# Attention with normed heads and a SiLU layer, in fp32: reciprocals spread in one round of DMAs, and whole products in the fillers of couples 4 to 8

## The chip, the cores and the metric

The program runs on one core of a Trainium2 chip. The metric is the device time of one execution in microseconds. Three runs of the kernel before took 1308.16, 1308.67 and 1309.16 us, so its median is 1308.67 us. Everything is computed in 32-bit floats.

The core's engines each work through their own list of instructions in order: PE (TensorE, matmuls), DVE (VectorE), ACT (ScalarE), POOL (GpSimd) and SP (SyncE, which here only issues DMAs). They wait for each other by semaphores.

## The reference

Two blocks follow each other: an attention with root-mean-square normed queries and keys, and a two-layer block with SiLU between.

```python
q, k, v: (8, 12, 448, 64)      # batch, heads, sequence, head dimension
def rmsnorm(x, g):
    return x / np.sqrt(np.mean(x * x, axis=-1, keepdims=True) + 1e-06) * g
q_n, k_n = rmsnorm(q, g_q), rmsnorm(k, g_k)
scores = 1.0 / np.sqrt(64) * np.matmul(q_n, k_n.transpose(0, 1, 3, 2))
attn = np.exp(scores - np.max(scores, axis=-1, keepdims=True))
attn = attn / (np.sum(attn, axis=-1, keepdims=True) + 1e-09)
out = np.matmul(attn, v)                         # (8, 12, 448, 64)
x = out.transpose(0, 2, 1, 3).reshape(3584, 768)
h = x @ w_in                                     # w_in: (768, 2048)
g = h * (1.0 / (1.0 + np.exp(-h)))
result = g @ w_out                               # w_out: (2048, 768)
```

## The kernel before

**Couples.** The 96 heads (8 batches of 12) are taken four at a time, as 24 "couples" of two pairs. Six couples (GROUP) make a group, the attention of two batches. For couple c, `visit(c)` computes the scores (L741, matmuls of 64 x 64), their exponentials on ACT (L746) and the product with v (L778); the last part of couple c-1's product with v, and its division by the row sums (L841, `divide`), lie in the visit of c. `between(c)` then prepares the next couple: it transposes queries and keys, adds up the exponentials (`add`, L792 on DVE; `sum_up`, L816, a matmul with ones on PE), takes the reciprocals (L825, in two halves on DVE) and spreads them.

**Spreading the reciprocals.** The sums come out as 32 rows for each combination of head h and pair i. `factors(c)` is a pair of tiles, one for each pair i, in which the reciprocals have to stand in both halves of the rows of a head. `spread` (L827 to L834) does so by DMAs of 32 x 448: four into the second tile (L832), and after these have landed, two within the first tile (L834). All are issued by SP, save that in couple 5 half of them go through POOL's queue.

**Fillers.** PE's work in the attention depends on ACT and DVE, so independent matmuls are put between: the first layer, x @ w_in, of the group before. They are products of Strassen's kind, seven for a block of 2 x 2 (class `Seven`: `two` makes products 1 and 2, `five` makes 6, 5, 7, 3 and 4). A product is three steps (HW), a step is one 128 x 128 x 448 fp32 matmul (two records in the trace, L940). The result of a product is emptied out of PSUM by DVE (`plus`, L890: an addition to a part already there) or by ACT (a copy, L948 or L958). In `five`, POOL adds product 5 to two parts (L960, L961), and products 3 and 4 are added to what results. `fill(others, prompt)` emits so many steps as are due (`filler["share"]`), and deals other work out between them. There are two fills in each `between`, except in couple 5, which has only one, before the group's end. From couple 6 on a fill is 13 steps, from 12 on 14. In couples 3 (second fill) to 5, `make_ahead` makes the products 1 and 2 of two blocks ahead, at 2.4 steps a fill.

**Where a product stands.** PSUM has two banks named "mm" for products, two places of two banks named "sc" (scores, transposes, sums from couple 6 on) and two for the product with v. `bank` gives a product an "mm" bank, or every second time an "sc" place if a flag allows: `turns["third"]`, set from couple 8 on, and only while more than five steps are due. In couples 8 to 10 it is off in the second fill.

**Generators.** A product yields after every step. The code that empties it stands after its last yield, so the emptying of a product that ends a fill is emitted when the next fill, or the work between, asks for a step.

**Other work.** `sum_x` (L887) adds parts of x, the left operands of the products. `Rounder` turns w_in (and w_out), which come as 64-bit words, into fp32: `load` (SP, L88), `open` (two ACT passes, L103 and L104), `round` (three DVE instructions, L126, L129, L133, and one on POOL, L137). `halves` says which of these come in which fill. `norm` squares, sums and scales the queries and keys: squares on ACT (L472), sums on DVE (L473), a power on POOL (L501), scaling (L516) for couple 7's q on POOL. `pair_up` (L726) writes a few small blocks by POOL before couple 8. After couple 23 the second layer's products ("deep", L1247 and L1284) run until the end.

All of this order is written out by hand: the instructions of an engine are those of the program text, in its order.

## Time and profile before

| | us |
|---|---|
| median of three runs | 1308.67 |
| the profiled execution | 1308.39 |
| its span | 1306.6 |
| PE busy | 1290.7 |
| DVE busy | 949.3 |
| ACT busy | 502.4 |
| POOL busy | 363.0 |

The granted clock of PE was 0.999 of full speed. The span is the time from the first to the last instruction of the profiled execution; the device time is 1.8 us more. A line of the timeline reads: start, duration, engine, source line, operation, the tile written and the tiles read, shapes, count, and in brackets how long the engine had been idle and what it waited for. "SPq" is SP issuing a DMA. Neighbouring instructions of one kind are put together, with their count behind the x. The attention, with its fillers, takes until about 725 us; couple 4's fills lie at 86.1 and 91.2 us, couple 5's at 110.6, couple 6's at 126.7 and 140.1, couple 7's at 162.0 and 173.5, couple 8's at 196.0 and 207.7, couple 9's at 230.1 and 241.0, couple 10's at 262.7 and 274.3.

### The profile page before, as it was taken

Reading aid. Unit: us, or ns where it says so; the run is one execution under the profiler, and the core shown is the slowest. Engines: PE = TensorE matmul, PEld = TensorE weight load, DVE = VectorE, ACT = ScalarE, POOL = GpSimd, SP = SyncE. Lnnn points to the kernel's source line nnn. Section 1 sums busy time; section 2 is a strip of 40 time slices with the busy share of each in tenths; the row PEclk is TensorE's granted clock in tenths of the full one; section 3 lists DMA queues with packets and bytes.
Section 4 is the critical chain, followed back from the end, with each engine's and each line's share of the span. In section 5 each row is a group of like instructions: output and inputs, shape, how many; then the busy total and the mean of one; then the engine's idle time right before and its main releaser. Section 6 shows DMA issues by size and latency. Waiting matters only on the chain.

```text
span 1306.6 us, 19889 instructions
## 1 busy us (share of the span) xinstructions
PE 1290.7 (99%) x7174; PEld 828.7 (63%) x7174; DVE 949.3 (73%) x1628; ACT 502.4 (38%) x880; POOL 363.0 (28%) x227
## 2 busy tenths in 40 slices
PE   8999999999999999999999999999999999999998
PEld 4444444444444444444444455558999999999998
DVE  6988777867555556755554786698978787878785
ACT  7866656655444545545534344310100000100000
POOL 6765555443334333334321244300000000000000
PEclk9999999999999999999999999999999999999999
DMA  8774347545444443444321457312323223231411
GB/s 209 194 194 134 102 98 189 129 99 124 95 97 93 123 95 89 111 106 93 87 77 48 155 178 260 117 61 83 102 83 101 89 90 102 76 127 51 137 42 40
DMA packets 267967, 146.32 MB, mean 112 GB/s; under 512 B 204356, under 2 KB 251748, under 8 KB 267860
## 3 DMA queue, kind: packets, MB, share of 16 engines
q1 hardware_dynamic: 267200, 143.80, 39.9%
q8 instruction: 59, 0.97, 0.3%
q0 software_dynamic: 352, 0.96, 0.2%
q14 instruction: 48, 0.39, 0.1%
q10 hardware_dynamic: 308, 0.20, 0.1%
HBM read 95.36 MB, written 41.29 MB: 105 GB/s over the span
## 4 chain that ended last, share of the span: by engine, by line
PE 90%; DVE 3%; ACT 2%; issue 2%; DMA 1%; SPq 1%; POOL 0%; ACTq 0%; DVEq 0%
PE alone L1247 23%; PE mm L940 18%; PE av L778 9%; PE sc L741 9%; PE sc L940 9%; PE mm L1247 8%; PE alone L940 7%; PE alone L1284 2%; PE mm L816 1%; PE sc L816 1%; DVE work L792 1%; PE mm L1284 1%; DMA rows<-in_k_dram 1%; ACT work L746 1%; PE sc L640 0%
## 5 line engine op out<-in xcount | busy, mean ns | idle before, releaser
L746 ACT ACTIVATE work<-sc,rms 128x448 f32<-128x448 f32 x318 | 181.3, 634 | 71.1 <-PE sc L741 54.0
L940 PE MATMUL mm<-x,W 128*128 128x448 f32 x396 | 163.4, 546 | 4.5 <-DVE stage L890 1.7
L741 PE MATMUL sc<-work 64*64 64x448 f32 x1344 | 164.0, 544 | 1.7 <-ACT work L746 0.8
L792 DVE TENSOR_TENSOR work<-work 128x896 f32<-128x896 f32 (+1 forms) x112 | 121.7, 1118 | 49.5 <-PE av L778 48.9
L778 PE MATMUL av<-work,rows 64*64 64x448 f32 x1272 | 150.3, 540 | 1.0 <-ACT av L754 0.7
L940 PE MATMUL mm<-sums_x,W 128*128 128x448 f32 x360 | 147.6, 543 | 0.5 <-DVE parts L890 0.5
L501 POOL TENSOR_TENSOR rms<-rms,minus_half 128x14 f32<-128x14 f32 (+4 forms) x40 | 95.9, 2400 | 133.9 <-DVE rms L497 128.7
L940 PEld LDWEIGHTS mm<-x,W 128*128 128x128 f32 x396 | 72.9, 190 | 85.6 <-issue 70.6
L528 POOL DMA_DIRECT2D out_dram<-x x2 | 1.2, 592 | 443.2 <-DVE x L890 443.2
L1247 PE MATMUL alone<-W,rows 128*128 128x192 f32 x610 | 113.1, 326 | 0.0
L940 PEld LDWEIGHTS mm<-sums_x,W 128*128 128x128 f32 x360 | 67.1, 190 | 72.3 <-issue 67.1
L778 PEld LDWEIGHTS av<-work,rows 64*64 64x64 f32 x1272 | 57.5, 132 | 69.5 <-issue 35.4
L1247 PEld LDWEIGHTS alone<-W,rows 128*128 128x128 f32 x610 | 101.5, 190 | 0.0
L741 PEld LDWEIGHTS sc<-work 64*64 64x64 f32 x1344 | 53.3, 132 | 71.3 <-ACT work L746 29.9
L717 POOL TENSOR_TENSOR rms<-rms,minus_half 128x28 f32<-128x28 f32 x15 | 71.9, 4791 | 67.4 <-DVE rms L714 61.0
L940 PE MATMUL sc<-x,W 128*128 128x448 f32 x216 | 87.9, 543 | 0.0
L960 POOL TENSOR_TENSOR parts<-parts,stage 128x448 f32<-128x448 f32 x31 | 41.5, 1338 | 148.3 <-DVE parts L890 147.9
L1247 PE MATMUL alone<-W,work 128*128 128x192 f32 x382 | 72.2, 326 | 0.0
L940 PEld LDWEIGHTS sc<-x,W 128*128 128x128 f32 x216 | 40.4, 190 | 42.9 <-issue 40.5
L1078 ACT ACTIVATE stage<-stage 128x896 f32<-128x896 f32 x63 | 57.3, 945 | 22.1 <-DVE stage L890 21.5
L1257 ACT COPY rows<-alone 128x192 f32<-128x192 f32 x33 | 10.5, 317 | 141.8 <-PE alone L1247 78.2
L1247 PEld LDWEIGHTS alone<-W,work 128*128 128x128 f32 x382 | 63.8, 190 | 0.0
(261 smaller groups left out, 2279.7 us busy)
## 6 DMA issues: line engine op xcount, KB each, us to landing
hidden<-stage SPq DMA_DIRECT2D x63, 448.0 KB, 3.1
work<-hidden SPq DMA_DIRECT2D x21, 1024.0 KB, 5.2
rows<-in_moe_w_out_dram SPq DMA_DIRECT2D x32, 384.0 KB, 3.6
W<-in_moe_w_in_dram SPq DMA_DIRECT2D x22, 512.0 KB, 5.1
x<-hidden SPq DMA_DIRECT2D x7, 1024.0 KB, 5.4
rows<-in_q_dram SPq DMA_DIRECT2D x120, 56.0 KB, 2.2
rows<-in_k_dram SPq DMA_DIRECT2D x120, 56.0 KB, 2.3
work<-work SPq DMA_DIRECT2D x111, 56.0 KB, 1.9
```

The source lines that it names most:

```text
L501: nc.gpsimd.tensor_tensor(out=t, in0=t, in1=half, op=ALU.pow)
L717: nc.gpsimd.tensor_tensor(out=f, in0=f, in1=minus_half.to_broadcast([P, n]), op=ALU.pow)
L741: nc.tensor.matmul(two[ds(half * D, D), h, 0:S], keys[rows, ts(half, D)], qT[rows, pair, :], start=True, stop=True,)
L746: nc.scalar.activation(left_weights(c)[:, h] if j == LEFT else weights(c, j)[:, i, h], two[:, h, 0:S], AF.Exp, scale=norm.column(c, i, h, j),)
L778: nc.tensor.matmul(sums[i][ds(h * D, D), :], v, w, start=(j == 0 and step == 1), stop=(j == LEFT - 1 and step == 1),)
L792: nc.vector.tensor_tensor(out=total, in0=total, in1=more, op=ALU.add)
L816: nc.tensor.matmul(t[ds(h * D + i * n, n), :], ones[:, which + i if which else 0], left_weights(c)[:, h] if which else w()[:, i, h], start ...
L940: nc.tensor.matmul(t, self.left(name, s), self.right(name, s), start=s == ends[0], stop=s == ends[1])
L960: nc.gpsimd.tensor_tensor(out=u2, in0=u2, in1=p5, op=ALU.add)
L1078: nc.scalar.activation(t, t, AF.Silu)
L1247: nc.tensor.matmul(t, x[:, i], y, start=i == ORDER[0], stop=i == ORDER[-1])
L1284: nc.tensor.matmul(o, a[:, 2 * i + m, t], right_one(name, i)[:, m], start=n == 0, stop=n == len(steps) - 1,)
```

## The change

- `spread`: from couple 5 on, DVE copies the first tile of reciprocals whole into the second (128 x 448), and then four DMAs, in one round, fill the rows that are wrong in each of the two. For earlier couples nothing changes but that all go through SP, as they did.
- Whole products: a `yield 0` stands after each emptying in `two` and `five`; `product` notes when the step just yielded was its last (`ended`), and `fill` then asks once more, so that the emptying is emitted in the same fill. `make_ahead` gets three steps in each of four fills.
- The third place: a product may go to "sc" in couples 6 and 7 while more than 5 and at most 10 steps are due, in couples 8 to 10 as before in the first fill, and in the second while more than 8 are due.
- `FULL` now holds couple 6 beside couple 10: there, too, the fourth piece of the exponentials is added up by PE (a further term of `sum_up`) and not by DVE.
- The sums over x of couple 6: two of the four steps stay in the visit; the other two go into the first fill, one before and one behind the additions and the words.
- The queries of couple 7: squares on ACT at the start of `between(5)`, scaling on DVE in the visit of couple 6 and not on POOL.
- The words: two openings at the start of `between(5)`, one round in couple 5's fill, one in the visit of couple 6. `pair_up` goes ahead of couple 7's second fill.
- In the deep products, one addition goes ahead of the emptying of product 7.

```diff
         def spread():
             mine = [a.rearrange("(h i p) s -> i h p s", h=2, i=2) for a in factors(c)]
             queues = (nc.sync, nc.gpsimd if c == GROUP - 1 else nc.sync)
+            if c >= EARLY:
+                nc.vector.tensor_copy(factors(c)[1], factors(c)[0])
+                for i in range(2):
+                    for h in range(2):
+                        queues[h].dma_start(mine[i][1 - i, h], mine[i][i, h])
+                return
             for h in range(2):
                 for i in range(2):
-                    queues[h].dma_start(mine[1][i, h], mine[0][1, h])
+                    nc.sync.dma_start(mine[1][i, h], mine[0][1, h])
             for h in range(2):
-                queues[h].dma_start(mine[0][1, h], mine[0][0, h])
+                nc.sync.dma_start(mine[0][1, h], mine[0][0, h])
...
-    FULL = SOON - 1
+    FULL = (GROUP, SOON - 1)
...
-        if c == FULL:
+        if c in FULL:
             terms.insert(0, (1, None))
...
     def bank(n):
         turn = turns["next"] = (turns["next"] + 1) % 4
-        if turns["third"] and filler["due"] > 5 * S and not turns["aside"]:
+        due = filler["due"] / S
+        if turns["least"] < due <= turns["most"] and not turns["aside"]:
...
                 if not (self.prompt and s == ends[1]):
+                    filler["ended"] = s == ends[1]
                     yield self.n
+            filler["ended"] = False
             return t
...
             plus((yield from self.product("6")), p1, u2)
+            yield 0
             nc.scalar.copy(p5, (yield from self.product("5")))
+            yield 0
             plus((yield from self.product("7")), u2, u3)
...
+        y = added(p5, out[1][1])
         plus(product(7), u2, u3)
         x = added(u3, out[1][0])
-        plus(u3, added(p5, out[1][1]), out[1][1])
+        plus(u3, y, out[1][1])
...
             step = next(filler["work"], None)
             if step is None:
                 break
+            if step == 0:
+                continue
             filler["due"] -= step
...
+        if filler["ended"]:
+            next(filler["work"], None)
         filler["due"] = min(filler["due"], 0.0)
...
+    halves[-2], halves[-1] = "r", ""
...
                 if c == GROUP:
-                    for steps in (range(2), range(2, 4)):
-                        for i in range(1, HW):
-                            sum_x(last_two(c), i, steps)
+                    for i in range(1, HW):
+                        sum_x(last_two(c), i, range(2))
+                    for i in range(2):
+                        norm.scale(c + 1, q_of(c + 1), q_of(c + 1), i, nc.vector)
+                    room.w_in.round()
...
         if c == GROUP - 1:
+            for _ in range(2):
+                room.w_in.open()
+            for i, t in enumerate(scratch):
+                size = z.R, 2 * J * D
+                rows = q_of(c + 2)[0 : z.R, ts(i, size[1])]
+                nc.scalar.activation(t[0 : size[0], 0 : size[1]], rows, AF.Square)
             transposes_and_sums()
...
-        if c >= GROUP and c != FULL:
+        if c >= GROUP and c not in FULL:
             late += add(c, LEFT)
         further = normalise(c + 2) if c >= GROUP - 1 else []
-        late += weights_in(c, 0) + (further[2:] if c >= GROUP else further[:2])
+        late += weights_in(c, 0)
+        if c == GROUP:
+            third, fourth = (
+                [lambda i=i, step=step: sum_x(last_two(c), i, (step,)) for i in range(1, HW)]
+                for step in (2, 3)
+            )
+            late = third + late + fourth
+        late += further[2:] if c >= GROUP else further[:2]
...
-        if c < SOON:
-            turns["third"] = False
+        if LATE - 1 <= c < SOON:
+            turns.update(least=8)
...
-            begin(make_ahead([0, 1]), AHEAD * 2 * HW * S, GROUP - 1)
+            begin(make_ahead([0, 1]), AHEAD * 2 * HW * S, AHEAD * 2)
         if c >= LATE - 2:
             if c == LATE - 2:
-                prompt.append(pair_up)
+                pair_up()
...
-        turns["third"] = c >= LATE - 1
+        turns.update(least=5 if c >= GROUP else 99, most=10 if c < LATE - 1 else 99)
         between(c)
```

More of the change, by code (lines that the diff above doesn't have):

```diff
@@ L468, in squares @@
         t = t[0 : rows.shape[0], 0 : rows.shape[1]]
-        if alone:
+        if alone is None:
+            pass
+        elif alone:
             nc.vector.tensor_tensor(out=t, in0=rows, in1=rows, op=ALU.mult)
@@ L851, in piece @@
             if name == "q":
-                norm.squares_q(c, source, t, i)
+                norm.squares_q(c, source, t, i, None if c == GROUP + 1 else False)
             else:
@@ L861, in piece @@
                 norm.root(c, name)
-                if name == "q":
+                if name == "q" and c != GROUP + 1:
                     for m in range(2):
@@ L912, in bounded @@
     ps_alone = None
-    turns = dict(next=0, aside=False, third=False)
-    filler = dict(work=iter(()), due=0.0, share=0.0)
+    turns = dict(next=0, aside=False, least=99, most=99)
+    filler = dict(work=iter(()), due=0.0, share=0.0, ended=False)
     def bank(n):
         turn = turns["next"] = (turns["next"] + 1) % 4
-        if turns["third"] and filler["due"] > 5 * S and not turns["aside"]:
+        due = filler["due"] / S
+        if turns["least"] < due <= turns["most"] and not turns["aside"]:
             turns["aside"] = True
@@ L943, in product @@
                 if not (self.prompt and s == ends[1]):
+                    filler["ended"] = s == ends[1]
                     yield self.n
+            filler["ended"] = False
             return t
         def two(self):
+            rest = self.n if self.prompt else 0
             nc.scalar.copy(self.p1, (yield from self.product("1")))
-            if self.prompt:
-                yield self.n
+            yield rest
             plus((yield from self.product("2")), self.p1, self.done[1, 1])
-            if self.prompt:
-                yield self.n
+            yield rest
         def five(self):
@@ L961, in five @@
             nc.gpsimd.tensor_tensor(out=done[2, 2], in0=u3, in1=p5, op=ALU.add)
+            yield 0
             plus((yield from self.product("3")), u2, done[1, 2])
+            yield 0
             plus((yield from self.product("4")), u3, done[2, 1])
+            yield 0
     stages = [stage[:, ts(i, 2 * S)] for i in range(3)]
@@ L1061, in halves_in @@
             for n in columns:
+                if n == 0:
+                    yield n
+                    continue
                 count += 1
@@ L1381, in fill @@
                 break
+            if step == 0:
+                continue
             filler["due"] -= step
@@ L1606, in bounded @@
         visit(c)
-        turns["third"] = c >= LATE - 1
+        turns.update(least=5 if c >= GROUP else 99, most=10 if c < LATE - 1 else 99)
         between(c)
-    turns["third"] = False
+    turns.update(least=99)
     visit(NC)
```

## The prediction

> **What bounds the kernel now.** I read the page first, then the waits of the matmul engine, then stretches of the timeline around each wait, then the busy times by fill.
>
> ```profile
> PE 1290.7 (99%) x7174; PEld 828.7 (63%) x7174; DVE 949.3 (73%) x1628; ACT 502.4 (38%) x880; POOL 363.0 (28%) x227
> PE 90%; DVE 3%; ACT 2%; issue 2%; DMA 1%; SPq 1%; POOL 0%; ACTq 0%; DVEq 0%
> ```
>
> PE is busy for 1290.7 of 1306.6 us, so only stalls of PE and matmuls added or removed can move the end. PE's waits, summed by cause (page's columns: total us, times, longest):
>
> ```profile
> PE mm L940 <- DVE parts L890: 1.9, 3, 0.8
> PE mm L940 <- DVE stage L890: 1.7, 4, 0.7
> PE mm L940 <- ACT stage L948: 0.8, 1, 0.8
> ```
>
> These, and one of 0.6 for ACT at L958, are the filler products (L940) waiting for a place in PSUM: with two "mm" banks, product n+2 waits for the copy or addition that empties product n. The modelled end of a matmul hides a part of each wait, so I count from start to start. Undisturbed records of L940 start 0.376 us apart; the first after a stall takes 0.104 more (0.644 against 0.539 long). One stall of couple 4's second fill (the "x2" stands for two records):
>
> ```profile
> 91.20 1.02 PE L940 MATMUL mm<-x,W 128*128 128x448 f32 x2
> 92.25 0.62 DVE L890 TENSOR_TENSOR stage<-mm,stage 128x448 f32<-128x448 f32 x1 [1.55 <-PE mm L940]
> 92.93 0.64 PE L940 MATMUL mm<-x,W 128*128 128x448 f32 x1 [0.72 <-DVE stage L890]
> ```
>
> The first record follows a 32-row matmul and takes 0.48 until the second; that one should be followed at 91.20 + 0.48 + 0.38 = 92.06 and is followed at 92.93: 0.87 of wait, with the restart 0.98. The product waited for had ended in the fill before; its addition stood behind this fill's first matmuls in program order. Done so for every gap, the fills lose: couple 4 0.98; couple 5 1.07; couple 6 1.05 + 0.79 + 0.10 = 1.94; couple 7 0.89 + 0.54 = 1.43; couple 8 0.86 and 1.29; couple 9 0.56. That is 8.1 us, and none in the fills of couples 10 to 23. The deep products from about 725 us on have no gap. So 8.1 us is all that this change could win in the fills.
>
> **The change, part by part.** Sums are against the profiled execution (1308.39 us, of which the span is 1306.6).
>
> *Whole products* (couple 3's second fill to couple 5: three steps per fill, not 2.4; and the addition of a product that ends a fill is issued at once). In couple 4 the addition now runs in the first fill, over 3 us before its bank is wanted: +0.98. In couple 5 this stood:
>
> ```profile
> 110.59 0.92 PE L940 MATMUL mm<-x,W 128*128 128x448 f32 x2
> 110.83 1.01 ACT L673 ACTIVATE work<-sc,gains 128x896 f32<-128x896 f32 x1
> 111.73 0.53 ACT L948 COPY stage<-mm 128x448 f32<-128x448 f32 x1
> 112.31 0.64 PE L940 MATMUL mm<-x,W 128*128 128x448 f32 x1 [0.81 <-ACT stage L948]
> ```
>
> ACT's copy of a finished product waited behind two ACT passes over the transposes. It now belongs to couple 4's second fill, and couple 5 has one product, whose bank is free: +1.07. The steps are only shared out anew, so PE's work is the same.
>
> *Couple 6.* The fourth piece's sum goes to PE: 4 matmuls with 32 rows (8 records, four side by side at 0.376) are 2 x 0.376 = 0.75 us more PE. DVE drops two L792 additions of 64x896 (1.09 each), which stood just ahead of the L890 that came late at 136.84. The sums over x are split: half stay in the visit, two L887 come before the first product's addition, two after the second's. In the visit q7's scaling goes from POOL to DVE (2 x 0.69, by L516's rows there). It also ends this:
>
> ```profile
> 121.53 2.10 POOL L516 TENSOR_TENSOR x<-x,rms 112x512 f32<-112x512 f32 x2
> 121.77 2.35 DVE L887 TENSOR_TENSOR sums_x<-x,sums_x 128x448 f32<-128x448 f32 x1
> ```
>
> The same L887 takes 0.62 alone: 1.73 lost here, 1.11 at the next beside L137. DVE's queue from the divides on (120.0): 4 L887 to 122.4, scaling to 123.7, one round of words (0.42 + 0.43 + 0.69) to 125.2, squares' sums and L792 to 128.6, two L887 to 129.7, the addition to 130.3, while its bank is wanted at 126.74 + 12 x 0.376 = 131.25. Before, it ended at 132.16. The third addition ends at 134.5 for a bank wanted at 135.8, as the product between stands in "sc". So all of 1.94 goes: +1.94 - 0.75 = +1.19. The round moved out of couple 5 frees 1.5 us of DVE there; the two openings moved earlier on ACT (2 x 1.35) and the squares (2 x 0.65) fall where ACT idles 3.61 us ahead of 110.03. Their pieces were loaded before. SP's order is unchanged but for the DMAs below.
>
> *Couple 7.* An addition that stood between the reciprocals now precedes them, and POOL's small copies (L726, 0.73) leave the front of L960. DVE then: reciprocals until 178.3, copy 0.38, words until 180.1, addition until 180.6; POOL still has L137 and then L960 until 182.7, the next addition ends at 183.3. Before, its bank came free at 183.91. Of 1.43 us I take +0.6, both stalls together.
>
> *The copy on DVE* (19 couples from 5 on, 128x448 fp32, SBUF to SBUF). No such row exists. Two near ones:
>
> ```profile
> L126 DVE TENSOR_SCALAR W<-W 128x512 f32<-128x512 f32 x24 | 10.7, 448 | 2.8 <-ACT W L104 2.7
> L1458 DVE COPY x<-av 128x448 f32<-128x448 f32 x10 | 5.8, 618 | 0.6 <-PE av L778 0.6
> ```
>
> L1458 reads PSUM (0.62, the upper end); L126 is one SBUF source to SBUF, like the copy: undisturbed 0.42 for 512, so 0.38 for 448. I take 0.38. Whether it also waits for POOL decides couple 8:
>
> ```profile
> 210.87 1.54 DVE L825 RECIPROCAL work<-sc 128x224 f32<-128x224 f32 x1
> 211.64 1.13 POOL L960 TENSOR_TENSOR parts<-parts,stage 128x448 f32<-128x448 f32 x1
> 212.73 1.14 POOL L961 TENSOR_TENSOR stage<-parts,stage 128x448 f32<-128x448 f32 x1
> 212.81 0.62 DVE L890 TENSOR_TENSOR stage<-mm,parts 128x448 f32<-128x448 f32 x1 [0.39 <-POOL parts L960]
> ```
>
> The copy would start at 212.4, inside L960. The Trainium skill ("GPSIMD Engine Reference", Specifications) says that POOL's SBUF interfaces are VectorE's too, with contention for DVE instructions in a two-port mode or with two SBUF inputs; "VectorE: DVE Perf Modes" (What auto-detection actually checks) puts an fp32 copy from SBUF to SBUF in the two-port mode. This speaks against the change. Held until both POOL additions end (213.87), the copy would end at 214.25 and the L890 queued behind it come 1.4 late: -1.4. But one row, of the same kind as the copy, got in between:
>
> ```profile
> 238.32 1.18 POOL L960 TENSOR_TENSOR parts<-parts,stage 128x448 f32<-128x448 f32 x1 [11.53 <-DVE parts L890]
> 238.54 1.24 DVE L129 TENSOR_SCALAR W<-W 128x512 int32<-128x512 int32 x1
> 239.45 1.32 POOL L961 TENSOR_TENSOR stage<-parts,stage 128x448 f32<-128x448 f32 x1
> ```
>
> It ended at 239.78, 0.28 after L960. By it the copy ends at about 213.1 and costs 0.25. I take -0.2 for couple 8's second fill, the third place helping a little elsewhere in it (bounds -1.4 to +1.29). Its first fill keeps its stall of 0.86. Couple 9: a bank more against 0.38 more of DVE, 0 (bounds -0.5 to +0.5). Couple 10: by the starts and ends in the trace, one product there finds its bank free 0.31 us ahead of time, which the copy eats: -0.2 (0 to -0.4). From couple 11 on the smallest such margin is 1.5 us, and DVE idles 1.4 to 2.5 us in each fill: 0. In four of those couples (12, 15, 18, 21) the copy begins inside L961 and waits 0.9; the kT transposition behind it comes 1.3 late, the addition after that 0.5, inside the margin.
>
> *The DMAs.* Four then two become four: 507 to 588 ns less of SP each, twice, and SP no longer waits for the first round to land (about 2 us). The factors are first used at the next couple's divides, over 5 us later, so that gains nothing by itself. But at 384.53 ACT's copy of a product had waited 3.56 us for "hidden<-stage" stuck in SP's queue behind the second round, and delayed the exps behind it: PE lost 0.24 at 388.13, and 0.20 at 689.96 I lay to the same. I take +0.2 of 0.44. *Deep products:* two additions swap on DVE, off PE's path; +0.1 at the tail.
>
> Sum: 0.98 + 1.07 + 1.19 + 0.6 - 0.2 + 0 - 0.2 + 0.2 + 0.1 = 3.7 us. The profiled execution becomes 1304.7; it lay 0.3 under the median of 1308.67, so the median becomes 1305.0.
>
> **Rivals.** (1) *DVE becomes the bound of couples 6 to 10.* In the couples' fills it is busy nearly throughout already (columns: PE, PEld, DVE, ACT, POOL busy):
>
> ```profile
> 126.74:138.37 11.63, 10.33 (x28) 4.75 (x27) 11.15 (x17) 4.33 (x8) 4.65 (x3) 1.00 0.18 61
> 240.95:251.38 10.43, 10.19 (x30) 4.85 (x27) 10.08 (x15) 9.05 (x13) 5.17 (x3) 1.00 0.32 78
> ```
>
> Shortened by the stalls, the fill has less DVE time than work. Then couple 6 wins only 1.0 - 0.75, couple 7 nothing, couple 8 loses 1.4, couple 9 0.5, couple 10 0.4: 0.98 + 1.07 + 0.3 - 2.3 + 0.3 = 0.4 won, 1308.3; half of it gives 1306.6. For it: the rows. Against it: L792, the round and contention go. (2) *All fill stalls go,* by the third place: 8.1 - 0.75 + 0.3 = 7.7, 1301.0. Against it: couples 8's first fill and its POOL chain are untouched. (3) *Slower: the copy is held for both POOL additions in every couple from 11 on.* Held 2.3 us plus 0.38, less the margin of 1.5, plus a restart of 0.1, it would cost 1.3 in each of 13 couples, 16.6 in all: 1321. It decides once the excess passes (3.7 + 2.6) / 13 = 0.5 us a couple. Against it: in the trace L960 overlaps the end of a reciprocal only in couple 8; elsewhere one L961 or nothing. (4) *The change doesn't do what it says:* couples 4 and 5 win, but ACT or DVE reach the early additions no sooner, and couple 6 only pays its 0.75: 2.05 - 0.75 = 1.3, 1307.4.
>
> **How the numbers follow.** My forecast 0.52 (1303.6 to 1306.0); rival 1 0.20 (1306.0 to 1308.7); rival 2 0.13 (1301.0 to 1303.5); rival 3 0.07; rival 4 0.08 (1306.0 to 1307.5). 0.2% is 2.6 us, about what a measurement of this kernel can tell from no change: faster means below 1306.05. That holds for the forecast, rival 2, a third of rival 1 at its halved form: 0.52 + 0.13 + 0.07 = 0.72; slower 0.07; the rest 0.21. The range runs from 1302.3 to 1307.6: it leaves out about half of rival 2, rival 3 and the worst of rival 1, some 2 in 10.
>
> **What would show it.** In the changed profile: no PE wait near 92 and 111; the L816 group of couple 6 with 16 records; no gap above 0.2 us in couple 6's fills; one gap of about 0.9 in couple 7's second fill, before an L890 that waits for L960; couple 8's two gaps still there; a new DVE copy group x19 near 0.38 mean, longer ones where POOL adds; no gap near 388. Wrong would be a forecast whose couple 6 keeps a gap over 0.5, whose copies average above 1 us, or where PE waits for L890 after couple 10.

## The result: 2.2 us won, where 3.7 were forecast

| | before | after |
|---|---|---|
| median of 20 runs, us | 1308.49 | 1306.33 |
| ratio, 95% interval | | 0.9985 (0.9978 to 0.9992) |
| profiled execution, us | 1308.39 | 1305.99 |
| its span, us | 1306.6 | 1304.2 |

The changed kernel is faster by 0.15%, clear of no change by its interval but inside the 0.2% that the prediction set as the bound of "faster" (1306.05): in that sense "faster", which it gave 0.72, did not come true. 1306.33 lies in the range (1302.3 to 1307.6), and just outside the likeliest case's own (1303.6 to 1306.0). The runs of both kernels scatter over 2 to 3 us (the last section has one reason), so single traces are compared below by where PE's matmuls start, stage by stage, and not by their ends alone.

### Where the time went

The two programs issue nearly the same matmuls in the same order. Pairing them and taking the difference of their starts (after minus before) gives an offset that changes only where something was won or lost:

| where | step of the offset, us | forecast |
|---|---|---|
| start of the kernel, until 33 us | -0.48 | - |
| visits 4 and 5 | +0.45 - 0.11 + 0.20 = +0.54 | 0 |
| couples 4 and 5, fills | -0.98 - 1.11 | -0.98 - 1.07 |
| couple 6, both fills and its sum | -1.05 - 0.78 + 0.75 - 0.10 = -1.18 | -1.19 |
| couple 7, second fill | -0.89 + 0.44 = -0.45 | -0.6 |
| couple 8, second fill | +0.27 | +0.2 |
| couple 9, second fill | -0.56 + 0.56 = 0 | 0 |
| couple 10 | 0 | +0.2 |
| visits 12, 15, 18, 21 | 4 x 0.21 = +0.84 | 0 |
| visits 13 to 23, other | about -0.05 | -0.2 |
| last matmul | -2.62 | |

The start isn't touched by the change. The traces of the other runs, whose start is unchanged too, lie 0 to 0.7 us later there than this one, and one lies 1.3 later, so its 0.48 is chance. Without it 2.14 us are left, close to the difference of the medians (2.16). That they agree so well is in part chance as well, for couple 10's step differs from trace to trace (below). What follows the last matmul took 0.2 us longer than in the trace before (span -2.4), where the swap of two deep additions had been put down at a gain of 0.1; in the traces of the other runs this tail takes 6.3 to 6.9 us, so neither can be told.

### The profile page after: what moved, and what is told of

The parts are those of the page before. It is cut to its first block, busy times and chain, and to the rows that moved or that the text cites. A ratio compares the mean times of both kernels' runs of the same rounds, so it can differ in the third digit from the quotient of the medians.

```text
span 1304.2 us, 19861 instructions
## 1 busy us (share of the span) xinstructions
PE 1289.4 (99%) x7182; PEld 831.2 (64%) x7182; DVE 958.3 (73%) x1647; ACT 502.2 (39%) x880; POOL 361.7 (28%) x224
## 4 chain that ended last, share of the span: by engine, by line
PE 80%; DVE 2%; ACT 1%; issue 0%; DVEq 0%; ACTq 0%
PE alone L1265 23%; PE mm L949 16%; PE sc L949 10%; PE mm L1265 8%; PE alone L949 7%; PE av L780 6%; PE sc L743 6%; PE alone L1303 2%; PE sc L818 1%; PE mm L1303 1%; DVE work L898 0%; ACT work L748 0%; ACT stage L1096 0%; DVE x L898 0%; DVE work L827 0%
## 5 line engine op out<-in xcount | busy, mean ns | idle before, releaser
L794 DVE TENSOR_TENSOR work<-work 128x896 f32<-128x896 f32 (+1 forms) x110 | 118.5, 1108 | 49.3 <-PE av L780 48.8
L949 PE MATMUL mm<-x,W 128*128 128x448 f32 x366 | 150.6, 544 | 2.6 <-DVE stage L898 2.0
L949 PE MATMUL mm<-sums_x,W 128*128 128x448 f32 x348 | 143.2, 543 | 0.3 <-DVE stage L898 0.3
L949 PEld LDWEIGHTS mm<-x,W 128*128 128x128 f32 x366 | 67.9, 190 | 75.4 <-issue 67.3
L949 PE MATMUL sc<-x,W 128*128 128x448 f32 x246 | 100.1, 543 | 0.0
L949 PEld LDWEIGHTS sc<-x,W 128*128 128x128 f32 x246 | 46.0, 190 | 48.9 <-issue 45.6
```

The lines of the kernel that those rows point to most:

```text
L794: nc.vector.tensor_tensor(out=total, in0=total, in1=more, op=ALU.add)
L949: nc.tensor.matmul(t, self.left(name, s), self.right(name, s), start=s == ends[0], stop=s == ends[1])
```

## The profile after

The page of the changed kernel, its busy times and its chain:

```profile
PE 1289.4 (99%) x7182; PEld 831.2 (64%) x7182; DVE 958.3 (73%) x1647; ACT 502.2 (39%) x880; POOL 361.7 (28%) x224
PE 80%; DVE 2%; ACT 1%; issue 0%; DVEq 0%; ACTq 0%
```

PE's instructions grew by the 8 records of couple 6's sum, DVE's by the 19 copies. PE is as full as before. PE's waits, summed by cause (total us, times, longest):

```profile
PE mm L949 <- DVE stage L898: 2.3, 3, 1.3
PE sc L743 <- ACT work L748: 1.0, 3, 0.4
PE mm L949 <- DVE parts L898: 0.6, 1, 0.6
PE av L780 <- ACT av L756: 0.5, 2, 0.3
```

The two waits for ACT's copies are gone, and of seven waits for DVE's additions four are left (three for L898 "stage", one for "parts"). The scores' wait for ACT went from 0.8 to 1.0. For ACT's L756 (L754 before) there are two waits of 0.5 together, where one of 0.7 stood; the one of 0.25 at visit 4 is new. The fills of couples 4 and 6 from the timeline: couple 4's product runs through, and couple 6's additions come when the prediction's queue had them.

```profile
91.81 2.52 PE L949 MATMUL mm<-x,W 128*128 128x448 f32 x6
...
127.56 0.61 DVE L898 TENSOR_TENSOR parts<-mm,stage 128x448 f32<-128x448 f32 x1
131.70 0.62 DVE L898 TENSOR_TENSOR parts<-mm,parts 128x448 f32<-128x448 f32 x1
```

The prediction ended these two at 130.3 and 134.5 in the times of the trace before; less the 2.03 won ahead of them, that is 128.27 and 132.47; they ended at 128.17 and 132.32. In couple 7 the one gap that was forecast stands, behind POOL's first addition:

```profile
178.45 1.13 POOL L972 TENSOR_TENSOR parts<-parts,stage 128x448 f32<-128x448 f32 x1
179.61 0.62 DVE L898 TENSOR_TENSOR stage<-mm,parts 128x448 f32<-128x448 f32 x1 [1.11 <-POOL parts L972]
180.29 1.02 PE L949 MATMUL mm<-x,W 128*128 128x448 f32 x2 [0.71 <-DVE stage L898]
```

The copy, by form (19 of them; mean in ns after the busy us), in couple 8, and in couple 12:

```profile
L833 DVE COPY work<-work 128x448 f32<-128x448 f32 x19 | 10.5, 555 | 0.6
...
208.12 1.13 POOL L972 TENSOR_TENSOR parts<-parts,stage 128x448 f32<-128x448 f32 x1
208.93 0.57 DVE L833 COPY work<-work 128x448 f32<-128x448 f32 x1
209.21 1.29 POOL L973 TENSOR_TENSOR stage<-parts,stage 128x448 f32<-128x448 f32 x1
...
339.83 1.12 POOL L973 TENSOR_TENSOR stage<-parts,stage 128x448 f32<-128x448 f32 x1
340.10 1.11 DVE L833 COPY work<-work 128x448 f32<-128x448 f32 x1
```

Fourteen took 0.39 (0.38 was taken). Couple 8's began inside POOL's first addition, ended 0.25 after that one, and POOL's second started in its turn: it was held by one addition, not by both. Four took 1.11, in couples 12, 15, 18 and 21, which are those that the prediction named: each began inside L973 and ran when that ended. So the price of meeting POOL is the rest of one POOL instruction.

### The two losses that were not forecast

*Visit 12* (and 15, 18, 21). First before, then after: the addition that empties the last product in an "sc" place, PE's next small matmul, and the first scores, which want that place.

```profile
315.27 0.61 DVE L890 TENSOR_TENSOR stage<-sc,parts 128x448 f32<-128x448 f32 x1
316.14 0.30 PE L713 MATMUL sc<-rms,ident 128*128 128x28 f32 x2
316.37 0.61 PE L741 MATMUL sc<-work 64*64 64x448 f32 x4
```

```profile
312.42 0.61 DVE L898 TENSOR_TENSOR stage<-sc,parts 128x448 f32<-128x448 f32 x1
312.75 0.30 PE L715 MATMUL sc<-rms,ident 128*128 128x28 f32 x2
313.18 0.98 PE L743 MATMUL sc<-work 64*64 64x448 f32 x8
```

Before, the addition ended 0.26 ahead of the small matmul and the scores came 0.23 behind it. After, it ends 0.28 behind it and the scores come 0.43 behind it. The copy in front of these visits (couples 11, 14, 17, 20) is the plain one of 0.39; what it delays is the kT transposition behind it, then ACT's scaling and squares, DVE's sums of them, and only then the addition. The prediction had set down as a sign of its being wrong that PE waits for this addition (L890, now L898) after couple 10: it does, at these four visits, though with the scores and not with a product.

*Visit 4.* In couple 3's second fill, ACT's copy of a product is now issued ahead of an opening of words. Before, then after:

```profile
71.72 0.70 ACT L104 ACTIVATE W<-W 128x512 f32<-128x512 f32 x1
74.20 0.53 ACT L948 COPY stage<-mm 128x448 f32<-128x448 f32 x1 [1.78 <-PE mm L940]
```

```profile
73.69 0.53 ACT L960 COPY stage<-mm 128x448 f32<-128x448 f32 x1 [2.93 <-PE mm L949]
74.12 0.69 ACT L103 ACTIVATE W<-W 128x512 int32<-128x512 uint32 x1
74.69 0.70 ACT L104 ACTIVATE W<-W 128x512 f32<-128x512 f32 x1
75.26 1.18 ACT L748 ACTIVATE work<-sc,rms 128x448 f32<-128x448 f32 x2
...
77.08 0.98 PE L780 MATMUL av<-work,rows 64*64 64x448 f32 x8 [0.25 <-ACT av L756]
```

ACT idles 2.93 us for the product, and the two passes that could have filled this time stand ahead of visit 4's exponentials.

## The experiments

Ratios are to the kernel before, run on the same chip. Expected microseconds are for a kernel before at 1308.5; its medians beside the three groups of runs were 1308.76, 1309.14 and 1308.66. "Step" means the offset of PE's starts to the changed kernel's trace.

| run | median | kernel before | ratio (interval) |
|---|---|---|---|
| two rounds everywhere | 1306.90 | 1308.76 | 0.9988 (0.9981 to 0.9995) |
| copy alone | 1310.54 | 1308.76 | 1.0013 (1.0006 to 1.0020) |
| late copy | 1310.07 | 1308.76 | 1.0009 (1.0002 to 1.0016) |
| early openings | 1306.36 | 1308.76 | 0.9984 (0.9977 to 0.9990) |
| copy behind the transposition | 1306.54 | 1309.14 | 0.9980 (0.9973 to 0.9986) |
| copy on ACT | 1310.15 | 1309.14 | 1.0005 (0.9996 to 1.0014) |
| couple 6's sum on DVE | 1306.68 | 1309.14 | 0.9980 (0.9972 to 0.9988) |
| q7's scaling on POOL | 1307.21 | 1309.14 | 0.9987 (0.9981 to 0.9994) |
| no third place in couples 6, 7 | 1307.22 | 1308.66 | 0.9992 (0.9986 to 0.9999) |
| couple 5 in two rounds | 1308.08 | 1308.66 | 0.9998 (0.9990 to 1.0007) |
| transposition first, openings early | 1306.33 | 1308.66 | 0.9985 (0.9978 to 0.9991) |
| the same, couples 7 to 9 in two rounds | 1304.45 | 1308.66 | 0.9969 (0.9957 to 0.9980) |

### Two rounds everywhere: is it the copy that costs at the visits?

```diff
-            if c >= EARLY:
-                nc.vector.tensor_copy(factors(c)[1], factors(c)[0])
-                ...
             for h in range(2):
                 for i in range(2):
-                    nc.sync.dma_start(mine[1][i, h], mine[0][1, h])
+                    queues[h].dma_start(mine[1][i, h], mine[0][1, h])
```

> The changed kernel with the old spreading of the reciprocals (four DMAs, then two) put back in all couples; all else stays changed. Theory A: the copy on DVE stands ahead of the kT transposition, so the addition that empties the last product in an sc place comes some 0.4 us later than before, and the first scores of visits 12, 15, 18 and 21, which want that place, lose 0.21 us each; the copy also eats 0.3 in couple 8's second fill and 0.4 to 0.5 in couple 9's. Without it these go: 0.84 + 0.3 + 0.45 = 1.6 us less; couple 13's gain of 0.1 is given back. About 1304.8 us (1306.33 - 1.5). Rival B: these losses come from the additions being issued earlier (whole products), not from the copy: the steps at visits 12, 15, 18 and 21 stay and the time is 1306.3.

The four steps went (-0.21, -0.21, -0.20, -0.21), so B falls: the copy costs them. Couple 7 won 0.51 and couple 8 0.34 (0.22 of it by a save that landed earlier, as the last section tells); couple 13's gain was given back (+0.25). Couple 9 won 0.04 where 0.45 was expected: its fill did win 0.49, but the first scores of visit 10 gave 0.45 of it back. They want the scaled keys, and ACT, which had no pause from the copy of a product at 241.95 on (a table load, the SiLU, the squares and an opening of words), scaled them last:

```profile
247.44 1.06 ACT L691 ACTIVATE work<-work,gains 128x896 f32<-128x896 f32 x1
248.55 0.98 PE L743 MATMUL sc<-work 64*64 64x448 f32 x8 [0.37 <-ACT work L691]
```

The late copy and the fastest version below show the same there (-0.47 and +0.41, -0.48 and +0.44).

A's time of 1304.8 didn't come, for visit 6 lost 1.0 us (1.1 with the next fill), which no theory had named. DVE's and SP's lines there:

```profile
115.36 0.51 SPq L836 DMA_DIRECT2D work<-work  x1
...
117.95 1.21 DVE L843 TENSOR_TENSOR x<-av,work 128x448 f32<-128x448 f32 x2 [1.65 <-DMA work<-work]
...
118.63 1.18 PE L780 MATMUL av<-work,rows 64*64 64x448 f32 x6 [0.23 <-DVE x L843]
```

The divide waits 1.65 us for the second round, and PE for the divide, which frees its accumulators. So what the new spreading wins in couple 5 and what it loses later nearly cancel: the ratio is 0.9988 without it and 0.9985 with it, and the intervals overlap. Nearly all of the 2.2 us comes from the other parts of the change.

### Couple 5 in two rounds: is that wait real?

```diff
-            if c >= EARLY:
+            if c > EARLY:
                 nc.vector.tensor_copy(factors(c)[1], factors(c)[0])
...
-                    nc.sync.dma_start(mine[1][i, h], mine[0][1, h])
+                    queues[h].dma_start(mine[1][i, h], mine[0][1, h])
...
-                nc.sync.dma_start(mine[0][1, h], mine[0][0, h])
+                queues[h].dma_start(mine[0][1, h], mine[0][0, h])
```

> The changed kernel with the old two rounds of DMAs in couple 5 alone. In the run with two rounds everywhere, visit 6 lost 1.0 us where the divide waited 1.6 us for the second round. Theory A: the one round pays in couple 5, where the visit follows the reciprocals soonest (one product between, not two): PE loses 0.8 to 1.0 at visit 6 and nothing elsewhere: 1307.2 if the kernel before is at 1308.5. Rival I: that wait was chance, from loads ahead of it: unchanged.

The steps are +1.07 - 0.27 at visit 6 and +0.34 in the fill behind it, as A has it; couples 7 to 9 have 0.1 or less. The wait of the divide is there again (1.68 us), so it isn't chance, and I falls. Couple 10 added 0.36, which other runs show too (below). The time was 1.75 over the changed kernel's, of which the steps give couple 5 1.14.

### Copy alone: what it costs without the rest

The kernel before, with the new `spread` as in the diff above the prediction.

> The kernel before with only the new spreading (copy on DVE from couple 5 on, one round of four DMAs). Theory A: slower, by 0.84 at the four visits 12, 15, 18 and 21, about 0.4 each in couples 7, 8, 9 and 10, where DVE's addition is what PE waits for, less 0.1 to 0.3 at couple 13: about 1310.7 us (1308.5 + 2.2). Rival B: the copy is hidden nearly everywhere and only couple 8 loses 0.3: 1308.8.

Slower by 1.8 us (1.0013), where A had 2.2 and B 0.3: A. The steps against the kernel before: couple 6 -0.30 + 0.47, couple 7 +0.49, couple 8 +0.31, couple 9 +0.39, visits 12, 15, 18 and 21 +0.21 each, couple 13 -0.34 + 0.17. In the order before, visit 6 found its reciprocals in time and won nothing from the one round. So the copy's price is about 2 us by the steps. What makes one round worth 1.1 in the changed kernel is another part of the same change: couple 5's stall is gone and its fill a step shorter, so visit 6 starts at 112.74 where it started at 114.77, while the old rounds' first DMA would be issued at 112.06 (two rounds everywhere) and not at 112.14. This is read from the three traces; no run lengthened the fill alone.

### The copy's place, three times

Late: from couple 7 on behind the transposition and the next addition.

```diff
-        yield [lambda: invert(0), lambda: (invert(1), spread())]
+        held = spreads.append if c >= LATE - 2 else lambda spread: spread()
+
+        yield [lambda: invert(0), lambda: (invert(1), held(spread))]
...
-            queries = prompt[3:] + [lambda: sum_squares(c + 2)]
+            queries = [lambda: spreads.pop()()] + prompt[3:] + [lambda: sum_squares(c + 2)]
...
```

> The changed kernel with the copy and its four DMAs issued three products' steps later from couple 7 on: behind the kT transposition and the next addition, ahead of the scaling and the sums of squares, where DVE has been idle for 0.5 to 1.4 us. Theory A: the copy's place is what costs: the steps of 0.21 at visits 12, 15, 18 and 21 go, and 0.3 to 0.4 each in couples 8 and 9: about 1304.8 us, and the divides of the next visit still find their reciprocals landed. Rival B: the place is immaterial (1306.3). Rival C: the reciprocals land too late for the next visit's divide, and PE waits at the first product with v of each visit: over 1307.

C came true (1.0009). The steps at the visits went (-0.21, -0.25, -0.21, -0.21), but visit 10 lost 2.7 us and more went at some later visits. SP's and DVE's lines:

```profile
246.24 5.95 SPq L255 DMA_DIRECT2D rows<-in_k_dram  x8
...
252.29 2.48 SPq L836 DMA_DIRECT2D work<-work  x4
...
255.03 0.62 DVE L851 TENSOR_TENSOR x<-av,work 128x448 f32<-128x448 f32 x1 [3.58 <-DMA work<-work]
```

The copy itself was done at 246.7, but its DMAs had slid behind the eight loads that the transposition sets free, 5.95 us of SP's queue. Behind the transposition but ahead of those loads:

```diff
-    def flip(c, name):
+    def flip(c, name, then=None):
...
         nc.vector.transpose(kT, place[z.BY_QUARTERS])
+        then()
         if c + 1 < NC:
             loads["quarters"](c + 1)
...
-        yield [lambda: invert(0), lambda: (invert(1), spread())]
+        held = spreads.append if LATE - 1 <= c < NC - 1 else lambda spread: spread()
+
+        yield [lambda: invert(0), lambda: (invert(1), held(spread))]
...
-                reciprocals += [lambda: flip(c + 1, "k"), gain]
+                reciprocals += [lambda: flip(c + 1, "k", spreads.pop()), gain]
...
```

> The changed kernel with the copy and its four DMAs moved from before the kT transposition to behind it (couples 8 to 22), ahead of the eight loads of keys that the transposition sets free on SP. Theory A: what costs at visits 12, 15, 18 and 21 is the transposition coming late (ACT's scaling and squares, and DVE's sums, follow it, and the last addition stands behind them): with the transposition first these steps of 0.21 go, 0.84 in all, and couples 8 and 9 gain at most 0.3: 1305.3 us. The reciprocals land 1 to 2 us later than in the changed kernel; in the late copy the wait for them (3.6 us at the visit of couple 10) came from the eight loads ahead of them on SP, which now stand behind. Rival B: DVE's whole work counts, not its order, so the steps stay: 1306.3. Rival C: the divides wait again: over 1307.

The steps at the visits went (-0.20, -0.24, -0.19, -0.21) and no divide waited in their place: A, and the transposition's place is the cause. But A's gain in couples 8 and 9 didn't come: couple 9 lost 0.20 and couple 10 0.17, in the trace of the first version below as well. The ratio is 0.9980 against the changed kernel's 0.9985; the intervals overlap, so the gain is shown by the steps and not by the time. (The profiled execution was the slowest of 21, with 1.3 us more at visit 4 and 2.3 in couple 8, where the clock dropped as the last section tells.)

On ACT, in the old place:

```diff
-                nc.vector.tensor_copy(factors(c)[1], factors(c)[0])
+                (nc.scalar.copy if c >= LATE - 2 else nc.vector.tensor_copy)(factors(c)[1], factors(c)[0])
```

> The changed kernel with the copy on ACT and not on DVE from couple 7 on, in the same place. Theory A: DVE's time in those fills is what is short: couple 7 gains 0.4 to 0.5, couple 8 0.3, the four visits 0.84 together; ACT is idle about 2.8 us ahead of the scaling of kT in the fills looked at, and takes about 0.55 for the copy: 1304.8 us. Rival D: ACT's later work (copies of products, squares) waits behind the copy for the reciprocal on DVE and gives it back: 1306.3 or more.

Both theories are seen: couple 7 won 0.44, couple 8 0.14 and the four visits 0.19 to 0.24 each; but couple 9 and the visit after it lost 4.4 us (1.5 of it by a lower clock behind the wait, as the last section tells), and visits 14, 17 and 20 0.3 each. D wins on the time. ACT's lines in couple 9, and PE's wait at its end:

```profile
242.34 0.56 ACT L833 COPY work<-work 128x448 f32<-128x448 f32 x1 [3.10 <-DVE work L827]
242.82 0.68 ACT L103 ACTIVATE W<-W 128x512 int32<-128x512 uint32 x1
...
247.49 0.93 ACT L698 ACTIVATE rows<-rows 128x896 f32<-128x896 f32 x1
248.45 1.09 DVE L704 TENSOR_REDUCE rms<-rows 128x28 f32<-128x896 f32 x1 [3.14 <-ACT rows L698]
...
249.69 0.38 PE L715 MATMUL sc<-rms,ident 128*128 128x28 f32 x2 [2.55 <-DVE rms L704]
```

ACT waited 3.10 us for the reciprocal, with an opening, a copy, the SiLU and the squares queued behind.

### Early openings

```diff
-        total = max(1, int(filler["due"] / S))
+        total = max(1, int(filler["due"] / S) - (filler["share"] < 5 * S))
```

> The changed kernel with the other work of the fills of couples 3 to 5 dealt out over one step fewer, as the kernel before did (it counted 2 of its 2.4 steps). Theory A: in couple 3's second fill ACT's copy of a product now stands ahead of an opening of words, so ACT idles 2.9 us for the product and the opening (two passes, 1.3 us) falls into visit 4 ahead of the exponentials; PE loses 0.45 there. With the opening ahead again this goes: 1305.9 us. Rival B: the copy itself delays the exponentials, whatever the order: unchanged, 1306.3.

The openings are ahead of the copy again, and the step at visit 4 is -0.43: A's cause holds. The median didn't move (1306.36), within what twenty runs that scatter over 3 us can tell; its profiled execution lost 2.5 us in couple 8 (last section).

### Couple 6's parts

```diff
-    FULL = (GROUP, SOON - 1)
+    FULL = (SOON - 1,)
```

> The changed kernel with the fourth piece of couple 6's exponentials added up by DVE again (two additions of 64x896, 1.09 each, in its first fill) and 8 matmul records fewer on PE. Theory A: PE gains 0.75 at the sum; the second product's addition (at 131.7 in the changed kernel's trace, its bank wanted at 133.75, margin 1.43) ends 2.2 later, so PE waits 0.75 and restarts for 0.1, and the third, wanted at 138.6, keeps its margin of 2.4: a wash, 1306.3. Rival E: the extra matmuls were needless, PE gains 0.7: 1305.6. Rival F: DVE's delay runs through both fills: 1307.5.

A came true: PE waited for the second product's addition (step +0.84) and won 0.75 at the sum. The work that the change moved to PE costs just what it saves.

```diff
-                        norm.scale(c + 1, q_of(c + 1), q_of(c + 1), i, nc.vector)
+                        norm.scale(c + 1, q_of(c + 1), q_of(c + 1), i, nc.gpsimd)
```

> The changed kernel with the scaling of couple 7's queries on POOL again, in the place where DVE now does it. Theory A: POOL's two multiplications (2.1 us) meet DVE's rounding behind them, whose instructions stretch from 1.5 us to some 3.5; DVE is spared 1.4 of scaling, so its queue is 0.6 us later at the first fill's additions, inside the margin of 1.4 us: PE's starts unchanged, 1306.3. Rival G: DVE and POOL don't disturb each other here, DVE is 1.4 us earlier, and PE's starts are unchanged too; the lengths of the rounding instructions tell.

DVE and POOL in the visit of couple 6:

```profile
119.94 2.66 POOL L518 TENSOR_TENSOR x<-x,rms 112x512 f32<-112x512 f32 x2
120.43 1.27 DVE L126 TENSOR_SCALAR W<-W 128x512 f32<-128x512 f32 x1
121.73 1.15 DVE L129 TENSOR_SCALAR W<-W 128x512 int32<-128x512 int32 x1
```

The two roundings take 1.27 and 1.15 beside POOL, 0.42 and 0.43 in the changed kernel; POOL's pair is stretched as well, from the 2.10 of the kernel before. They take turns: each side waits for the other's instruction in hand. The page "SBUF — State Buffer" of the Trainium skill (section "SBUF: two separate sides") calls it an exclusive lock for the whole instruction, between a POOL operation and a DVE one in a two-port mode or with two SBUF inputs; these lengths agree. DVE ended 0.5 later, so G falls, and PE lost 0.32 where A said 0: not at an addition but at the product in the "sc" place. That place comes free with the exponentials, which waited for DVE's additions (L794) and so came late.

```diff
-        turns.update(least=5 if c >= GROUP else 99, most=10 if c < LATE - 1 else 99)
+        turns.update(least=5 if c >= LATE - 1 else 99, most=99)
```

> The changed kernel with no product in an sc place in couples 6 and 7 (couples 8 and later as changed). From the changed kernel's trace, each product would then wait for the second one ahead: in couple 6's second fill product 7, due at 143.12, for an addition that ends at 143.44: 0.4 with its restart; in couple 7's second fill the one due at 177.16 for 177.50, 0.45, which the next wait of 0.89 there takes up. Theory A: 0.4 to 0.5 us in all, 1306.8 if the kernel before is at 1308.5. Rival H: the third place was what took couples 6 and 7's stalls away: more than 1.5 us.

The step at product 7 is +0.54, and in couple 7 the wait was taken up as said (-0.01): A. Couples 8 and 10 added 0.48 and 0.35 without having been touched: couple 8 because a save landed later in this execution (last section), couple 10 as in four other runs with the same fill.

### Two versions to beat both kernels

Transposition first and openings early:

> The changed kernel with the copy behind the kT transposition (couples 8 to 22) and the openings of couple 3's second fill ahead of ACT's copy: steps of -0.84 in all at visits 12, 15, 18 and 21, and -0.43 at visit 4. Theory A: both add up, ratio to the kernel before 0.9975 against the changed kernel's 0.9985 (1305.2 if the kernel before is at 1308.5). Rival J: what is won at visit 4 is lost again in couple 8, where ACT waits for a save of hidden values that comes behind loads in SP's queue: 0.998.

The trace has both (-0.47 at visit 4; -0.20, -0.24, -0.19, -0.21 at the visits), and its end is 0.73 ahead of the changed kernel's. A's ratio of 0.9975 didn't come, though: ten of 21 runs lie below 1306, but the median is the changed kernel's. J can't be told from chance here: visit 4's gain was still there after couple 8 in this trace.

In couples 7, 8 and 9 also the old two rounds, without a copy:

```diff
-            if c >= EARLY:
+            if c >= EARLY and not GROUP < c < LATE + 1:
...
-        yield [lambda: invert(0), lambda: (invert(1), spread())]
+        held = spreads.append if LATE + 1 <= c < NC - 1 else lambda spread: spread()
+
+        yield [lambda: invert(0), lambda: (invert(1), held(spread))]
...
```

> The kernel of the run with copy behind the transposition and early openings, and in couples 7, 8 and 9 the old two rounds of DMAs and no copy: the copy's cost of 0.5 in couple 7 and 0.3 in couple 8 goes, couple 5 keeps its one round. Theory A: 0.8 us below the run beside it, ratio to the kernel before 0.997 (1304.5 if the kernel before is at 1308.5). Rival K: SP's second round delays the saves of hidden values that ACT waits for in couple 8, and gives it back: 0.9975 or more.

A came true: 0.9969 (0.9957 to 0.9980, from seven runs), 4.2 us below the kernel before, with steps of -0.45 at visit 4, -0.49 in couple 7, -0.25 in couple 8 and -0.82 at the visits. Of the kernels run it is the fastest, with nearly twice the changed kernel's gain. It lies 1.9 below the run beside it, where A said 0.8; the two traces differ by 1.2 from couple 7 on, for the 0.20 that the later copy lost in couple 9 and 0.14 in couple 10 are back as well. The other 0.7 these traces don't explain.

## Why the prediction was partly right

**By the number alone** the forecast's own interval was missed: 1306.33 lies in those of rivals 1 and 4. What the forecast had right and wrong is seen from the steps.

**Right.** That the stalls of couples 4 to 6 go, with their sizes: 0.98, 1.07 (1.11) and 1.19 (1.18). Couple 6's queue on DVE was worked out to within 0.15 us, and moving the sum to PE was indeed paid for by the stall that it removes. The copy's length (0.39), the four couples where it waits for L961, and that it gets in between POOL's two additions in couple 8 (0.2 forecast, 0.27 measured) held: the row L129 was the better guide than the case of a copy held for both. In couple 8, though, only 0.12 of the 0.27 are the copy's; the rest is a save that landed later (last section). Rival 3, the slower one, is out by the same rows, and rival 4 by couples 4 to 6. Rival 2 (all fill stalls go) is out too: beyond the usual 0.376, gaps of 0.87 in couple 7, 0.74 and 1.46 in couple 8 and 0.49 in couple 9 are left. That couples 4 and 5 win by the whole products is read from the traces before and after; no run takes them out again, nor the split sums over x or the deep swap.

**Wrong: "From couple 11 on the smallest such margin is 1.5 us: 0".** This step took the margin of the "mm" banks alone. A product also stands in an "sc" place, and what comes next to that place isn't a product but the next visit's scores. The chain to its addition runs through the transposition behind the copy. Before, that addition ended 0.49 us before the first scores; against the small matmul beside it, it comes 0.54 later after the change, and each time this costs 0.21 (0.84 in all, where the term was 0). The runs without the copy, and with it behind the transposition, show that.

**Wrong: nothing was put down for what early emptying costs.** The whole products were costed on the banks that come free sooner. The prediction did not name what is queued behind ACT's copy, once it is issued in the fill and waits there for PE: an opening, then the exponentials of visit 4 (0.45 less 0.11, shown by the early openings), and in couple 4 the copy itself ahead of visit 5's (0.20, argued from the trace only).

**Mis-sized: couple 7 (0.6 forecast, 0.45 measured).** The mechanism, an addition that waits for L960, held; there the copy costs 0.49 to 0.51 by three runs.

**Wrong in its reason: "The factors are first used ... over 5 us later, so that gains nothing by itself".** In couple 5, where the visit comes 2 us earlier after the change, the second round would come 1.65 us late; the one round is worth 1.1 us there. It was worth nothing in the order before, which is the trace that I read. That couple 5's gain of 1.07 came out as forecast was therefore luck in part: the change uncovers a wait of about the same size, which I had not seen, and the one round, which I had put at nothing, takes it away. Of the 0.2 put down for the freer SP queue about 0.14 came at 388 and nothing at 690.

**Not settled by one trace: couple 10.** 0.2 was forecast, 0 measured in the changed kernel's trace, and 0.27 to 0.36 in five other runs with the same fill.

Rival 1 (DVE becomes the bound) was wrong in couple 6. In couple 8 the copy costs 0.12 to 0.13, not the 1.4 of that rival. In couple 9 the copy does take 0.4 to 0.5 of the fill, but without it ACT's scaling of the keys holds PE for as long, so there neither engine alone is the bound.

## What to carry to other kernels

When work is put ahead of something in an engine's queue, take the margin of every resource that the queue behind it frees, with the next user of each: the scores here, not only the next product. Ask it in the order that the change makes, not in the old one: a wait that is hidden today can be uncovered by another part of the same change. And where an emptying instruction is issued early, look at what stands behind it while it waits.

## What the runs showed of the hardware that was not expected

**A stall of PE of 2.1 us and more cost twice, for the clock dropped behind it.** In couple 8 ACT's copy of product 5 waits for a save of hidden values that stands in SP's queue behind the loads of v: 3.2 to 4.4 us in every trace. DVE's sums, reciprocals, copy and additions follow it, and PE waits for an addition in the second fill. So the landing of this save sets couple 8's step. In the runs with couple 6's sum on DVE, q7's scaling on POOL, couple 5 in two rounds and no third place, whose couple 8 is the changed kernel's, ACT's copy starts 0.13 and 0.07 earlier and 0.11 and 0.49 later against PE than in the changed kernel, and the steps are -0.13, -0.07, +0.11 and +0.48. Taken off in the same way, 0.15 of the changed kernel's +0.27, 0.22 of the 0.34 won with two rounds everywhere and 0.18 of the 0.31 lost by the copy alone are this, and what is left, 0.12 to 0.13 each time, is the copy on DVE.

First ACT's wait and PE's in the run with early openings, in its slowest execution (1309.07); then the busy times of the stretch behind that wait (columns: PE, PEld, DVE, ACT, POOL, and then PE's granted clock, the DMA share, GB/s), in this run and in the changed kernel.

```profile
203.13 0.53 ACT L969 COPY stage<-mm 128x448 f32<-128x448 f32 x1 [4.42 <-DMA hidden<-stage]
213.90 3.32 PE L949 MATMUL mm<-x,W 128*128 128x448 f32 x5 [2.27 <-DVE stage L898]
214.50:218.00 3.50, 3.50 (x8) 1.64 (x6) 0.34 (x1) 1.98 (x3) 0.23 (x1) 0.53 0.65 106
```

```profile
214.50:218.00 3.50, 3.50 (x30) 1.61 (x32) 0.72 (x2) 2.40 (x4) 1.45 (x1) 1.00 0.81 109
```

Behind the gap the granted clock is 0.53, and four records take 0.75 where 0.376 is usual: 1.5 us more on top of a wait that was 1.0 longer than the changed kernel's. In the fourteen traces, PE's gaps from start to start were followed by this at 2.51, 2.81 and 3.09 us (the run with the copy behind the transposition, this one, and the copy on ACT), and not at 2.32, 2.02, 2.00 and below. The page "TensorE: Matmul & The Clock Gate" of the Trainium skill (Part 1) has the clock halved after an idle window of about 3.4 us; here 2.13 us beyond the usual 0.376 were enough (1.94 were not), so the measurement decides.

For this change that matters: in the kernel before, couple 8's second fill lost its time in three small gaps (longest 1.06 from start to start), in the changed kernel in one of 1.84. A save that lands a little later brings it over the edge. Four of the changed kernel's twenty runs lie 1.49 us or more above its median. That these are such executions is argued, since its own trace isn't one. The clock granted over a whole execution bears it out in part: two of the four (1308.45 and 1308.83) have 0.998 and 0.997, the other two 0.999, as most have. In the run without a third place the four slowest (1309.48 to 1309.78, all others at most 1307.56) have 0.997. The fastest version's gap there is 1.54.

**POOL and DVE took turns by whole instructions** where DVE read and wrote SBUF: a copy of 0.39 took 1.11 from within one POOL addition and 0.57 near the end of one with another queued, and POOL's own pair went from 2.10 to 2.66. An addition that reads PSUM wasn't held: 0.62 beside L961 (at 212.81 in the trace before), as elsewhere.
